# Talking-heads attention into a squared-ReLU feed-forward: three score blocks, eight gather tiles, and first loads in two batches

## The chip, the cores and the metric

The kernel runs on one core of one Trainium2 chip. The metric is device time in microseconds (us). A profiled execution also gives a trace; its span is the time from the first to the last instruction, a little less than the device time.

## The reference

There are 8 batches of 12 heads, 448 queries and keys, and a head dimension of 64. Attention mixes heads twice: the scores of the 12 heads are mixed by w_pre ahead of the softmax, and the softmax by w_post after it. A feed-forward layer with squared ReLU follows (768 to 2048 to 768).

```python
scores = scale * np.matmul(q, k.transpose(0, 1, 3, 2))
scores = np.einsum('bhij,hg->bgij', scores, w_pre)
attn = softmax(scores)                                  # over keys
attn = np.einsum('bhij,hg->bgij', attn, w_post)
x = np.matmul(attn, v).transpose(0, 2, 1, 3).reshape(B * S, H * D)
h = np.maximum(x @ w_in, 0.0)
out = h * h @ w_out
```

## The kernel before

**Data.** A score block holds 120 (the last of a batch: 88) queries of all 12 heads, queries on partitions. Mixing heads needs heads on partitions, so each tile of 10 queries is gathered: a DMA (gather, L344) copies 10 rows of 12 heads from the score block `S` to 120 partitions of a gather tile `G`. A batch has 45 such tiles in four blocks of 12, 12, 12 and 9.

**One iteration.** The main loop runs over `ds`, two tiles at a time, 180 times and two more. In this text, iteration n is the pass with ds = n. Tiles are numbered through all batches, so iteration n mixes tiles 2n and 2n + 1, and batch 1 starts with tile 45. An iteration issues, in this order:

- the loads due (POOL's DMA queue; `at_load(i, ...)` is due when i is 2 ds or 2 ds + 1)
- timed units, such as `av_unit` (attention times v: ot_ps, L195)
- `unmix` of two tiles (L385): w_post is applied with the softmax tile `d` as the weights; DVE copies the result to `at` (L390). It stands LAG = 2 iterations behind mix
- in three iterations per batch `turn_unit` (L178): q and k of a later batch are transposed on PE and copied by DVE and ACT (L182)
- `scores_for`: score pairs, two heads each. `score_pair` runs 4 matmuls (L324) and two copies into the block, one on ACT and one on DVE (L327)
- `mix` (L353): w_pre is applied to two gather tiles. ACT takes the exponential with its sum (L358), DVE the reciprocal (L360), POOL scales it into a `d` tile (L362)
- `gathers_for`: the gathers that are due
- `spin` in the first ten iterations: matmuls without use that keep PE busy
- `fill`: units of the feed-forward of an earlier batch, from a list `filler`: `ffn1_unit` (h_ps, L246; ACT or DVE takes the ReLU, POOL or DVE the square, L258) and `ffn2_unit` (o_ps, L279; DVE copies it, L286 or L291, and SP's queue stores it, L269 or L294). Their share per iteration is set by the code's weights and not by the lines that change.

The order on PE and POOL is that of the code, since the loop stands in a manual schedule. Each other engine also works in the order in which its instructions were issued. PSUM has eight banks, taken in turn by all units.

**What paces scores and gathers.** There are 32 blocks of 6 pairs. `needs(step)` says how many pairs must have been issued for a tile. `gathers_for(ds)` issues gathers up to tile 2 ds + AHEAD + 1, with AHEAD = 10, and stops at a tile whose block isn't complete. There are AHEAD + 2 = 12 gather tiles, used in turn. `scores_for` sets how many pairs are wanted from the block that the gathers are in, with cases of its own for the first twelve iterations and for the turn from batch 0 to batch 1 (`FIRST_TURN`), and issues one or two per iteration. Score blocks have two buffers (`bufs=2`). The third block of batch 0 is held in a third place, the tile that later takes the second half of the weights w_out (`shared_half`, w2_1), so the loads of that half stand after its gathers.

**Queues.** POOL issues all loads of q, k, v and weights; these are DMAs that also cast, on queue q0 of the profile. Gathers go on SP's queue (q1), in batch 0 every second one on ACT's (q10). SP also issues the stores. A DMA from SP or ACT waits, before it is issued, for the eighth DMA before it from those two, as these share eight semaphores; POOL's have eight of their own.

**Start.** q and k of batch 0 are loaded and turned, and six pairs are issued as the parts arrive. Then come the first gathers (tiles 0 to 9), six more pairs, a spin of 8 rounds (32 matmuls), and all loads marked -1: four parts of v (192 KB each) and eight of w_in (`w1`, 384 KB each).

Of the kernel before, what the change touches and what calls it, by code (L numbers as in the profile page):

```python
# [1 line left out]

# [6 lines left out]
BF16 = mybir.dt.bfloat16  # L9
# [14 lines left out]
NT = 45  # L24
# [6 lines left out]
TW = TQ + 2  # L31
PARTS = [[0, 16, 32, NT], [0, 15, 31, NT]]
LAG = 2
AHEAD = 10
OFF = 64 - H * (IQ // 2)
SCALE = 1.0 / 8.0
FIRST_TURN = (15, 16, 17)
# [6 lines left out]
def kernel(  # L44
# [76 lines left out]
    onesblk = consts.tile([P, 64], BF16, name="onesblk")  # L121
    nc.vector.memset(onesblk[:, :], 1.0)

    ND = 2 * LAG + 4
    DW = S + PR
    dts = [consts.tile([P, DW], BF16, name=f"d{x}") for x in range(ND)]
    for t in dts:
# [14 lines left out]
    half2 = FT // 2 * DMODEL  # L142
    w2 = {0: wts.tile([P, half2], BF16, name="w2_0")}

    def shared_half():
        return wts.tile([P, half2], BF16, name="w2_1", tag="w2_1", bufs=1)

    def w2_part(x):
        return w2[x][:, :].rearrange("p (c m) -> p c m", m=DMODEL)


    qTs, kTs, bvecs, xts, h2ts, ats = {}, {}, {}, {}, {}, {}

# [77 lines left out]

    def load_w2(x):
        n = DFF // 8
        c = x % 4 * 2
        if x == 4:
            w2[1] = shared_half()
        nc.gpsimd.dma_start(out=w2_part(x // 4)[:, c:c + 2, :],
                            in_=moe_w_out[n * x:n * x + n, :].rearrange("(c p) m -> p c m", p=P))

    def ffn1_unit(b, ft, half, c0=0, c1=S):  # L240
        if half == 0:
            h_open[0] = bank("h_ps")
        ps = h_open[0]
        n = c1 - c0
        for c2 in range(3 * half, 3 * half + 3):
            nc.tensor.matmul(ps[:, 0:n], lhsT=w1[ft // 4][:, c2, ft % 4 * 128:ft % 4 * 128 + 128],  # L246
                             rhs=xts[b][:, c2, c0:c1], start=(c2 == 0), stop=(c2 == NPAIR - 1))
        if half == 0:
            return
        if (b, ft) not in h2ts:  # L250
            h2ts[(b, ft)] = ffnp.tile([P, S], BF16, name="h2", tag="h2", bufs=FT + 1)
        hr = ffnp.tile([P, S], F32, name="hr", tag="hr", bufs=2)
        if n < S and ft % 2:
            nc.vector.tensor_scalar_max(out=hr[:, 0:n], in0=ps[:, 0:n], scalar1=0.0)
        else:
            nc.scalar.activation(out=hr[:, 0:n], in_=ps[:, 0:n], func=ACT.Relu)  # L256
        square = nc.vector if n < S and ft % 4 else nc.gpsimd
        square.tensor_tensor(out=h2ts[(b, ft)][:, c0:c1], in0=hr[:, 0:n], in1=hr[:, 0:n], op=ALU.mult)  # L258

    h_open, o_open, osbs = {}, {}, {}  # L260
# [11 lines left out]
    def ffn2_unit(b, mt, nt, part):  # L272
        if part == 0:
            o_open[(b, mt, nt)] = bank("o_ps")
        ps = o_open[(b, mt, nt)]
        for ft in range(4 * part, 4 * part + 4):
            for n2 in ((nt,) if mt < 3 else (0, 1)):
                dst = ps[:, 0:384] if mt < 3 else ps[64 * n2:64 * n2 + 64, 0:384]
                nc.tensor.matmul(dst, lhsT=h2ts[(b, ft)][:, mt * 128:mt * 128 + ROWS[mt]],  # L279
                                 rhs=w2_part(ft // 8)[:, ft % 8, n2 * 384:(n2 + 1) * 384], start=(ft == 0), stop=(ft == FT - 1))  # L280
        if part < 3:
            return
        if mt < 3:
            if nt == 0:
                osbs[b] = ffnp.tile([P, DMODEL], F32, name="osb", tag="osb", bufs=2)
            nc.vector.tensor_copy(out=osbs[b][:, 384 * nt:384 * nt + 384], in_=ps[:, 0:384])  # L286
            if nt == 1:
                store_rows(b, mt, osbs[b])
        else:
            osb = ffnp.tile([P, 384], F32, name="osb3", tag="osb3", bufs=1)  # L290
            nc.vector.tensor_copy(out=osb[:, :], in_=ps[:, 0:384])  # L291
            r, p = divmod(128 * mt, PR)
            for n2 in range(2):
                nc.sync.dma_start(out=out_rows[b, r, p:p + 64, n2 * 384:(n2 + 1) * 384],  # L294
                                  in_=osb[64 * n2:64 * n2 + 64, :])
# [15 lines left out]
    def score_pair(n):  # L311

        b, blk, p = n // (4 * NPAIR), n // NPAIR % 4, n % NPAIR
        if (b, blk) not in Sb:
            if (b, blk) == (0, 2):
                Sb[(b, blk)] = shared_half()[:, 0:H * S].rearrange("p (h s) -> p h s", s=S)
            else:
                Sb[(b, blk)] = work.tile([P, H, S], BF16, name="S", tag="S", bufs=2)
        pss = [bank("s_ps") for _ in range(2)]
        for hh in range(2):  # L320
            rs = slice(64 * hh, 64 * hh + 64)
# [14 lines left out]
    def gather(k):  # L336

        b, t = steps[k]
        blk, tl = divmod(t, TPB)
        n = min(IQ, S - IQ * t)  # L340
        x = BLK_OFF[blk] + IQ * tl
        g = gts[k % len(gts)]
        eng = nc.scalar if b == 0 and k % 2 else nc.sync
        eng.dma_start(out=g[OFF:OFF + H * n, :], in_=Sb[(b, blk)][x:x + n, :, :])  # L344
        Gs[k] = g

# [72 lines left out]
    with tc.manual_schedule(engines={PE, POOL}):  # L419
# [12 lines left out]
        for x in range(2):  # L432
            at_load(-1, load_w1, x)
        for x in range(4):
            at_load(-1, load_v, 0, x)
            at_load(44 + x, load_v, 1, x)
        for x in range(2, 8):
            at_load(-1, load_w1, x)
        for x in range(8):
            at_load(18 + 2 * x + (6 if x > 3 else 0), load_w2, x)  # L440
        for x in range(6):
            at_load(6 + 2 * x, load_qk, 1, x)
            at_load(46 + 2 * x, load_qk, 2, x)
        for b in range(1, B):
            if b + 2 < B:
                for x in range(6):
# [2 lines left out]
                for x in range(4):  # L449
                    at_load(NT * b + 34 + 2 * x, load_v, b + 1, x)  # L450
        nd = len(steps) // 2
        issued, gathered = [2 * NPAIR], [0]
        blocks = [(b, blk) for b in range(B) for blk in range(4)]
        starts = [NT * b + TPB * blk for b, blk in blocks] + [len(steps)]

        def scores_for(ds, most):
            tile = 2 * ds + AHEAD + 2
            blk = sum(tile >= x for x in starts) - 1
            if blk + 1 >= len(blocks):
                want = NPAIR * len(blocks)  # L460
            elif ds < 2 * NPAIR:
                want = 2 * NPAIR + 1 + ds
            elif blk in (3, 4):
                want = NPAIR * 4 + 2 * max(0, ds - FIRST_TURN[0])
            else:
                into, size = tile - starts[blk] - 2, starts[blk + 1] - starts[blk] - 2
                want = NPAIR * (blk + 1) + -(-NPAIR * into // size)
            want = min(want, issued[0] + most, NPAIR * min(blk + 2, len(blocks)))
            k = min(2 * ds + 8, len(steps) - 1)
            want = max(want, needs(steps[k]))  # L470
            while issued[0] < want and issued[0] % NPAIR < turned.get(issued[0] // (4 * NPAIR), 0):
                score_pair(issued[0])
                issued[0] += 1
# [6 lines left out]
                gathered[0] += 1  # L480

        gathers_for(-1)
        for n in range(NPAIR, 2 * NPAIR):
            score_pair(n)
        spin(8)
        for f in loads.get(-1, []):
            f()
        for ds in range(nd + LAG):
# [82 lines left out]
```

## Time and profile before

| What | Before |
|---|---|
| median of 4 runs | 610.61 us (609.32 to 612.82) |
| profiled execution: its time / its span | 608.88 / 607.1 us |
| busy PE / DVE / ACT / POOL | 554.4 / 426.0 / 412.2 / 396.9 us |
| mean granted PE clock | 0.979 |
| DMA | 74.99 MB, mean 124 GB/s |
| gathers G<-S | 105 KB each; SP takes 0.78 us to issue one, ACT 0.80 us |

PE is TensorE, DVE is VectorE, ACT ScalarE, POOL GpSimd and SP SyncE; PEld is PE's weight load. An engine's line is shown as "start, length, engine, line, operation, tile written <- tiles read, count [idle time before it <- what ended that]". An engine can be idle at no cost when it isn't the one that sets the end. A queue's share is the time that its packets took, as a share of the 16 DMA engines in the stretch; it can sum to over 1, as packets of several queues are under way at once. Granted clock is a share of full speed.

### The profile page before, as it was taken

How to read it: one execution, taken by the hardware profiler on the slowest of the kernel's cores; microseconds unless marked ns; L12 is line 12 of the kernel's file. 1: busy time of each engine (PE TensorE's matmuls, PEld its weight loads, DVE VectorE, ACT ScalarE, POOL GpSimd, SP SyncE). 2: the span in 40 equal slices, each digit the busy share in tenths (PEclk: the TensorE clock that was granted, in tenths of full speed). 3: DMA queues.
4: the chain of work that ended last, by engine and by line, in shares of the span. 5: the costliest groups of instructions: out<-in, count | busy, mean ns of one | idle time of the engine just before them, and what ended most of it. 6: DMA issues, size and time to landing. Idle time of an engine off the chain costs nothing.

```text
span 607.1 us, 28400 instructions
## 1 busy us (share of the span) xinstructions
PE 554.4 (91%) x11922; PEld 313.6 (52%) x11922; DVE 426.0 (70%) x1104; ACT 412.2 (68%) x1217; POOL 396.9 (65%) x587
## 2 busy tenths in 40 slices
PE   3698787789899999999999999999999999999997
PEld 1365555545455455545555455545555555555554
DVE  5488697988787777786787687777777777755101
ACT  3377575676689767886688667886688767962420
POOL 7278556557468954997469944996468845892440
PEclk9899797999899999999999999999999999999999
DMA  9999769669555786388546785388544665432103
GB/s 137 226 199 215 152 108 175 123 102 170 131 116 119 137 157 138 66 152 148 121 109 116 143 160 131 62 166 137 127 100 87 111 151 119 79 66 56 38 11 81
DMA packets 83364, 74.99 MB, mean 124 GB/s; under 512 B 6436, under 2 KB 80164, under 8 KB 83236
## 3 DMA queue, kind: packets, MB, share of 16 engines
q1 hardware_dynamic: 48982, 47.20, 33.0%
q0 software_dynamic: 31264, 23.60, 28.6%
q10 hardware_dynamic: 2990, 2.37, 1.2%
q8 instruction: 93, 1.52, 1.0%
q14 instruction: 35, 0.29, 0.1%
HBM read 47.20 MB, written 11.01 MB: 96 GB/s over the span
## 4 chain that ended last, share of the span: by engine, by line
PE 67%; POOL 9%; DVE 9%; DMA 5%; ACT 4%; issue 2%; ACTq 0%; DVEq 0%
PE o_ps L279 24%; PE h_ps L246 17%; PE at_ps L385 8%; PE ot_ps L195 7%; PE m_ps L353 5%; DVE at L390 5%; DMA G<-S 4%; POOL d L362 4%; POOL h L258 3%; PE s_ps L324 3%; PE tr_ps L178 2%; ACT e_sb L358 2%; ACT xt L206 1%; POOL qkst L71 1%; DVE S L327 1%
## 5 line engine op out<-in xcount | busy, mean ns | idle before, releaser
L362 POOL TENSOR_SCALAR d<-e_sb,rc 128x448 bf16<-128x448 f32 x360 | 228.1, 645 | 164.9 <-DVE rc L360 163.2
L390 DVE CAST at<-at_ps 128x480 bf16<-128x480 f32 x360 | 219.8, 650 | 58.9 <-PE at_ps L385 53.7
L358 ACT ACTIVATE e_sb<-m_ps 128x448 f32<-128x448 f32 x360 | 196.0, 559 | 13.9 <-PE m_ps L353 6.5
L246 PE MATMUL h_ps<-xt,w 128*128 128x448 bf16 (+2 forms) x960 | 164.6, 319 | 2.1 <-DVE at L390 0.7
L279 PE MATMUL o_ps<-w,h 128*128 128x384 bf16 (+1 forms) x1024 | 162.9, 329 | 0.9 <-ACT xt L206 0.5
L327 ACT CAST S<-s_ps 128x448 bf16<-128x448 f32 x186 | 96.4, 542 | 54.5 <-PE s_ps L324 33.0
L246 PEld LDWEIGHTS <-w 128*128 128x128 bf16 x960 | 80.7, 99 | 77.7 <-issue 27.8
L279 PEld LDWEIGHTS <-h 128*128 128x128 bf16 (+1 forms) x1024 | 83.0, 101 | 71.9 <-issue 26.9
L258 POOL TENSOR_TENSOR h<-hr 128x448 bf16<-128x448 f32 (+2 forms) x124 | 108.7, 884 | 17.1 <-ACT hr L256 17.1
L327 DVE CAST S<-s_ps 128x448 bf16<-128x448 f32 x186 | 110.8, 614 | 4.6 <-DMA G<-S 4.6
L353 PE MATMUL m_ps<-G,pre 64*64 64x448 bf16 x720 | 82.0, 360 | 13.5 <-DVE at L390 3.3
L385 PEld LDWEIGHTS <-d 60*64 60x64 bf16 x5760 | 64.6, 109 | 55.6 <-issue 31.4
L385 PE MATMUL at_ps<-post,d 60*64 60x60 bf16 x5760 | 85.5, 195 | 6.8 <-POOL d L362 3.2
L256 ACT ACTIVATE hr<-h_ps 128x448 f32<-128x448 f32 (+2 forms) x136 | 68.8, 514 | 23.5 <-PE h_ps L246 11.2
L360 DVE RECIPROCAL rc<-sm 128x1 f32<-128x1 f32 x360 | 52.3, 156 | 39.9 <-ACT e_sb L358 37.8
L324 PE MATMUL s_ps<-kT,qT 64*64 64x448 bf16 x768 | 70.7, 372 | 9.2 <-ACT S L327 7.8
L358 ACT ACTIVATION_READ_ACCUMULATOR e_sb<-m_ps 128x1 f32 x360 | 78.5, 218 | 0.0
L206 ACT ACTIVATE xt<-ot_ps,bvec 128x160 bf16<-128x160 f32 (+3 forms) x144 | 44.8, 385 | 48.9 <-PE ot_ps L195 39.5
L286 DVE COPY osb<-o_ps 128x384 f32<-128x384 f32 x48 | 26.0, 547 | 39.9 <-PE o_ps L279 39.5
L195 PE MATMUL ot_ps<-at,v 128*64 128x160 bf16 (+4 forms) x1152 | 47.2, 233 | 5.1 <-ACT S L327 2.6
L195 PEld LDWEIGHTS <-v 128*64 128x64 bf16 x1152 | 39.6, 112 | 18.3 <-issue 17.6
L353 PEld LDWEIGHTS <-pre 64*64 64x64 bf16 x720 | 29.0, 107 | 33.5 <-issue 28.2
(43 smaller groups left out, 227.9 us busy)
## 6 DMA issues: line engine op xcount, KB each, us to landing
G<-S SPq DMA_DIRECT2D x324, 105.0 KB
out_dram<-osb SPq DMA_DIRECT2D x48, 192.0 KB
v<-in_v_dram POOLq DMA_DIRECT2D x32, 192.0 KB, 5.4
qkst<-in_k_dram POOLq DMA_DIRECT2D x24, 224.0 KB, 6.0
qkst<-in_q_dram POOLq DMA_DIRECT2D x24, 224.0 KB, 5.4
w<-in_moe_w_in_dram POOLq DMA_DIRECT2D x8, 384.0 KB, 18.4
w<-in_moe_w_out_dram POOLq DMA_DIRECT2D x8, 384.0 KB, 14.4
G<-S ACTq DMA_DIRECT2D x16, 105.0 KB
```

Source lines behind the costliest of these rows:

```text
L195: nc.tensor.matmul(ps[64 * hh:64 * hh + 64, TW * y + c0:TW * y + 2 + n], lhsT=vs[b][:, g, r, :], rhs=at[:, r, g, c0:2 + n], start=(y == 0 ...
L246: nc.tensor.matmul(ps[:, 0:n], lhsT=w1[ft // 4][:, c2, ft % 4 * 128:ft % 4 * 128 + 128], rhs=xts[b][:, c2, c0:c1], start=(c2 == 0), stop=( ...
L256: nc.scalar.activation(out=hr[:, 0:n], in_=ps[:, 0:n], func=ACT.Relu)
L258: square.tensor_tensor(out=h2ts[(b, ft)][:, c0:c1], in0=hr[:, 0:n], in1=hr[:, 0:n], op=ALU.mult)
L279: nc.tensor.matmul(dst, lhsT=h2ts[(b, ft)][:, mt * 128:mt * 128 + ROWS[mt]], rhs=w2_part(ft // 8)[:, ft % 8, n2 * 384:(n2 + 1) * 384], sta ...
L324: nc.tensor.matmul(pss[hh][z:z + 64, 0:S], lhsT=qTs[b][rs, p, q0:q0 + 64], rhs=kTs[b][rs, p, :], start=True, stop=True)
L327: copy(out=Sb[(b, blk)][:, 2 * p + hh, :], in_=pss[hh][:, 0:S])
L353: nc.tensor.matmul(pss[y][64 * x:64 * x + 64, 0:S], lhsT=pre[rows, :], rhs=gs[x][rows, :], start=True, stop=True)
L358: nc.scalar.activation(out=e[:, :], in_=pss[y][:, 0:S], func=ACT.Exp, scale=SCALE, accum_out=sm[:, 0:1])
L362: nc.gpsimd.tensor_scalar(out=d[:, 0:S], in0=e[:, :], scalar1=rc[:, 0:1], scalar2=-1.0 / S, op0=ALU.mult, op1=ALU.add)
L385: nc.tensor.matmul(us[x][PR * z:PR * z + PR, c:c + HR], lhsT=d[rows, j:j + PR], rhs=post[rows, :], start=True, stop=True)
L390: nc.vector.tensor_copy(out=dst, in_=src)
```

## The change

It has these parts:

- `S` has three buffers. w_out lies in four tiles of its own, so no score block shares its place.
- AHEAD goes from 10 to 6, so there are 8 gather tiles. The number of `d` tiles goes from 8 to 6. The tile osb3 is gone; the last rows use the tile osb.
- Scores are paced by `place(tile)`, the pair count, with fractions, that belongs to a tile's place in its block, taken at tile 2 ds + AHEAD + LEAD (20 ahead). The special cases are gone. Two pairs are issued in an iteration when the issue is behind by more than 1.5 (2 where a timed unit stands), else one, and never more than three blocks from the one being gathered.
- Nine pairs are issued ahead of the loop where there were twelve, and six gathers where there were ten. The first spin has 4 rounds.
- ACT issues only gathers 1 and 3.
- Of the loads marked -1 only two parts of w1 and two of v remain. The others are due in iterations 1 to 4, those of q and k of batch 1 from iteration 4 (before: 3), and those of w_out one per iteration from 10 to 17 (before: 9 to 12 and 16 to 19).
- The squares of batch 0 go to DVE for ft % 2, where they went for ft % 4; so 8 of 16 and not 4 of 16 are POOL's in each part of the batch.

```diff
-AHEAD = 10
+AHEAD = 6
+LEAD = 14
...
-    ND = 2 * LAG + 4
+    ND = 2 * LAG + 2
...
-    w2 = {0: wts.tile([P, half2], BF16, name="w2_0")}
...
+    w2 = [wts.tile([P, FT // 4, DMODEL], BF16, name=f"w2_{x}") for x in range(4)]
...
-        square = nc.vector if n < S and ft % 4 else nc.gpsimd
+        square = nc.vector if n < S and ft % 2 else nc.gpsimd
...
-            osb = ffnp.tile([P, 384], F32, name="osb3", tag="osb3", bufs=1)
-            nc.vector.tensor_copy(out=osb[:, :], in_=ps[:, 0:384])
+            osb = ffnp.tile([P, DMODEL], F32, name="osb", tag="osb", bufs=2)
+            nc.vector.tensor_copy(out=osb[:, 0:384], in_=ps[:, 0:384])
...
-            if (b, blk) == (0, 2):
-                Sb[(b, blk)] = shared_half()[:, 0:H * S].rearrange("p (h s) -> p h s", s=S)
-            else:
-                Sb[(b, blk)] = work.tile([P, H, S], BF16, name="S", tag="S", bufs=2)
+            Sb[(b, blk)] = work.tile([P, H, S], BF16, name="S", tag="S", bufs=3)
...
-        eng = nc.scalar if b == 0 and k % 2 else nc.sync
+        eng = nc.scalar if k in (1, 3) else nc.sync
...
-            at_load(-1, load_v, 0, x)
+            at_load(-1 if x < 2 else 2, load_v, 0, x)
             at_load(44 + x, load_v, 1, x)
         for x in range(2, 8):
-            at_load(-1, load_w1, x)
+            at_load(1 + x, load_w1, x)
+        for x in range(6):
+            at_load(9 + 2 * x, load_qk, 1, x)
+            at_load(46 + 2 * x, load_qk, 2, x)
         for x in range(8):
-            at_load(18 + 2 * x + (6 if x > 3 else 0), load_w2, x)
-        for x in range(6):
-            at_load(6 + 2 * x, load_qk, 1, x)
-            at_load(46 + 2 * x, load_qk, 2, x)
+            at_load(20 + 2 * x, load_w2, x)
...
-        issued, gathered = [2 * NPAIR], [0]
+        issued, gathered = [NPAIR + 3], [0]
...
-        def scores_for(ds, most):
-            tile = 2 * ds + AHEAD + 2
+        def place(tile):
             blk = sum(tile >= x for x in starts) - 1
             if blk + 1 >= len(blocks):
-                want = NPAIR * len(blocks)
-            elif ds < 2 * NPAIR:
-                want = 2 * NPAIR + 1 + ds
-            elif blk in (3, 4):
-                want = NPAIR * 4 + 2 * max(0, ds - FIRST_TURN[0])
-            else:
-                into, size = tile - starts[blk] - 2, starts[blk + 1] - starts[blk] - 2
-                want = NPAIR * (blk + 1) + -(-NPAIR * into // size)
-            want = min(want, issued[0] + most, NPAIR * min(blk + 2, len(blocks)))
-            k = min(2 * ds + 8, len(steps) - 1)
-            want = max(want, needs(steps[k]))
+                return NPAIR * len(blocks)
+            return NPAIR * (blk + (tile - starts[blk]) / (starts[blk + 1] - starts[blk]))
+
+        def scores_for(ds, most):
+            want = math.ceil(place(2 * ds + AHEAD + LEAD))
+            full = sum(gathered[0] >= x for x in starts) - 1
+            want = min(want, issued[0] + most, NPAIR * min(full + 3, len(blocks)))
+            want = max(want, needs(steps[min(2 * ds + 4, len(steps) - 1)]))
...
-        for n in range(NPAIR, 2 * NPAIR):
+        for n in range(NPAIR, issued[0]):
             score_pair(n)
-        spin(8)
+        spin(4)
...
-                scores_for(ds, 2 if ds < NT // 2 or not now and ds % 3 == 0 else 1)
+                behind = place(2 * ds + AHEAD + LEAD) - issued[0]
+                scores_for(ds, 2 if behind > (2 if now else 1.5) else 1)
```

More of the change, by code (lines that the diff above doesn't have):

```diff
@@ L1 @@
+import math
 from contextlib import ExitStack
@@ L141 @@
     w1 = [wts.tile([P, NPAIR, DFF // 4], BF16, name=f"w1_{x}") for x in range(4)]
-    half2 = FT // 2 * DMODEL
-    w2 = {0: wts.tile([P, half2], BF16, name="w2_0")}
[L145 to L149, printed above, removed]
+    w2 = [wts.tile([P, FT // 4, DMODEL], BF16, name=f"w2_{x}") for x in range(4)]
     qTs, kTs, bvecs, xts, h2ts, ats = {}, {}, {}, {}, {}, {}
@@ L233, in load_w2 @@
         n = DFF // 8
[L234 to L237, printed above, removed]
+        c = x % 2 * 2
+        nc.gpsimd.dma_start(out=w2[x // 2][:, c:c + 2, :],
                             in_=moe_w_out[n * x:n * x + n, :].rearrange("(c p) m -> p c m", p=P))
@@ L279, in ffn2_unit @@
                 nc.tensor.matmul(dst, lhsT=h2ts[(b, ft)][:, mt * 128:mt * 128 + ROWS[mt]],
-                                 rhs=w2_part(ft // 8)[:, ft % 8, n2 * 384:(n2 + 1) * 384], start=(ft == 0), stop=(ft == FT - 1))
+                                 rhs=w2[ft // 4][:, ft % 4, n2 * 384:(n2 + 1) * 384], start=(ft == 0), stop=(ft == FT - 1))
         if part < 3:
@@ L294, in ffn2_unit @@
                 nc.sync.dma_start(out=out_rows[b, r, p:p + 64, n2 * 384:(n2 + 1) * 384],
-                                  in_=osb[64 * n2:64 * n2 + 64, :])
+                                  in_=osb[64 * n2:64 * n2 + 64, 0:384])
     def ffn1_units(b, c0=0, c1=S):
```

## The prediction

> **What bounds the kernel now.** I read the busy time by stretches first, then the waits of TensorE (PE), the chain of waits and the queues. Columns of the stretches: stretch, its length, then busy us (instructions) of PE, weight loads, DVE, ACT, POOL, then granted clock, DMA share, GB/s.
>
> ```profile
> 0.00:20.00 20.00, 9.38 (x242) 5.36 (x246) 13.27 (x49) 7.49 (x12) 13.45 (x25) 1.00 1.06 152
> 20.00:40.00 20.00, 13.62 (x326) 8.87 (x318) 9.43 (x27) 11.41 (x34) 8.66 (x15) 0.83 1.06 216
> 40.00:60.00 20.00, 16.53 (x490) 11.36 (x485) 17.60 (x52) 15.62 (x51) 16.42 (x26) 1.00 1.10 216
> ...
> 80.00:100.00 20.00, 15.14 (x318) 10.53 (x319) 17.27 (x48) 11.96 (x39) 12.33 (x20) 0.93 0.86 143
> ...
> 300.00:400.00 100.00, 97.75 (x2202) 52.68 (x2190) 75.56 (x188) 79.44 (x233) 72.94 (x106) 1.00 0.62 122
> ```
>
> From about 160 us to 550 us PE is 97 to 99% busy at full clock. What is left to win lies ahead of that: PE idles some 30 us before 160 us, part of it at a lower clock, while the DMA engines are full for the first 60 us. A delay removed there moves the end by the same amount, since PE then works through a fixed list. The longest pieces of the chain (start, length, what) show where the idle time is:
>
> ```profile
> 16.82 8.20 DMA G<-S
> ...
> 56.01 7.41 DMA G<-S
> ...
> 92.43 5.46 DMA G<-S
> ...
> 147.77 5.06 DMA G<-S
> ```
>
> All are gathers, but of two kinds. The first is mixing waiting for its first tiles. The last two are score copies that wait until a score block is free, as the waits there show:
>
> ```profile
> 98.21 0.53 ACT L327 CAST S<-s_ps 128x448 bf16<-128x448 f32 x1 [4.86 <-DMA G<-S]
> 98.79 2.50 PE L195 MATMUL ot_ps<-at,v 128*64 128x128 bf16 x43 [2.63 <-ACT S L327]
> ```
>
> ACT works in order: its score copy waits 4.86 us for a gather of the old block, and everything behind it, then PE, waits too. The same occurs at 152.93 (2.29 us on ACT, 1.99 us on PE).
>
> The queues, first from 24 to 36 us, then from 92 to 98 us (packets, MB, share of 16 engines):
>
> ```profile
> q0 software_dynamic: 1339, 1.32, 65.2%
> q1 hardware_dynamic: 764, 0.63, 20.3%
> q10 hardware_dynamic: 759, 0.63, 15.6%
> ```
> ```profile
> q0 software_dynamic: 1326, 0.70, 93.6%
> q1 hardware_dynamic: 486, 0.40, 23.7%
> ```
>
> q0 carries POOL's loads, q1 the gathers of SP, q10 those of ACT. With both q1 and q10, 12.7 gathers of 120 packets pass in 12 us: 0.95 us each. With SP alone beside loads, 4.05 pass in 6 us: 1.5 us each.
>
> **What the Trainium skill says.** "DMA: Bandwidth & Descriptors", Queues, rings and completion order: each DMA engine takes its rows in turn, packet by packet. The trace fits. A packet takes 65.2% x 192 / 1339 = 93 ns on q0, 51 on q1, 40 on q10. By the same page (Why a DMA increments its semaphore by 16) a gather from 10 score rows runs on 10 engines, so 12 packets on each: an estimate of 12 x (93 + 51 + 40) = 2.2 us for a pair of gathers; the trace has 1.9. For q1 alone, 92 to 98 us: 12 x (68 + 47) = 1.4 us per gather; the trace has 1.5. The section Issuing engines are not separate DMA queues says a second issuer saves issue time only; under load the two windows speak against that, as two rows get two turns. "TensorE: Matmul & The Clock Gate", What's actually happening: an idle PE falls to half clock. The trace has 12 h_ps matmuls (128x128) in 1.48 us after the wait at 98.8 us; before, 12 of 128x160 took 1.00.
>
> **The change part by part.** "Iteration" is one pass of the ds loop (two tiles). I count the mixes in the timeline: mix 0 starts at 26.46 us, 9 at 45.99, 10 at 49.63, 14 at 58.05, 15 at 63.55, 17 at 70.45, 22 at 87.76, 24 at 93.80, 25 at 102.30, 34 at 129.63, 43 at 154.05. Which pair and gather falls in which iteration follows from the arithmetic of scores_for and gathers_for.
>
> (a) First loads and ACT's queue. Before, ACT issues its fourth gather and is then held until 25.83 (ACTq 17.70, 8.13 us x4) as a DMA waits for an earlier one. Its next score copy starts at 25.87, mix 0 at 26.46. After, ACT issues two gathers, only six are started at once, and 6 w1 parts and 2 v parts are left for later. q0 then has 6 qk, 2 w1 and 2 v parts: 6 x 0.23 + 2 x 0.39 + 2 x 0.2 = 2.56 MB; the stretches moved 102 GB/s in the first 10 us and 201 in the next 10, so they end near 18 us. Gathers start at 16.82 as before and land in about 4.5 us (estimate; the chain's 5.06 and 5.46 had loads beside them): mix 0 at 21.3. Gain 5.2. Bounds 2 (only the ACT hold goes) and 6.
>
> (b) The same loads later, past POOL's queue and beside gathers. Iterations 1 to 4 issue v, v, w1 / w1, w1 / w1, w1 / w1, qk on POOL ahead of that iteration's two d (0.63 us each, L362). A load costs POOL 0.65 to 0.77 us. So POOL needs 2.1 + 1.3, 1.5 + 1.3, 1.5 + 1.3, 1.4 + 1.3 = 11.7 us for four iterations that took 2.0 each: by POOL alone, d of iteration 9 starts some 3.9 us earlier than now, 1.3 less than 5.2. Then the gathers: all but two go on q1 alone. While q0 has work, one takes 12 x (93 + 51) = 1.73 us, a pair 3.5, against iterations of 2.0. Eight tiles land before that starts, at about 24 us; tile 19 then lands at 24 + 12 x 1.73 = 45 and mix 9 starts near 46: all of (a) lost. In iterations 10 to 17 one w2 part is issued in each, where before four were in iterations 9 to 12. With w2 packets (76.8% x 208 / 1408 = 113 ns) a gather takes 1.97 us, and 16 of them 31.5: mix 17 at 77.5, 7 later than now. That is the far end (-12); the near end is -1.3. q0 is not always full (68.6% of the engines from 36 to 48 us, where qk parts came one by one), so I take -3.5.
>
> (c) Squares of batch 0: ft % 2 in place of ft % 4 moves 4 of 16 squares per part, 12 in all, from DVE (0.42 us) to POOL (0.45): 5 us off DVE, 9 to 10 of 10 us busy from 80 to 120 us; POOL has room there (5 to 7). A fifth of it on the path: +1 (0 to 2).
>
> (d) First gathers of batch 1. Before, tile 45 is gathered in iteration 19 (82.25 us), after it in iteration 20, as pairs come two at a time: pairs 28, 29 copied by about 85, landing 4.5 later at 89.5, mix 22 due at 87.76. DVE has fewer copies just before, so I take -1.3 (0 to -2.3).
>
> (e) Third score block. No pair now waits for its buffer: the first pair of a block comes five or more iterations after the last gather from the buffer it takes (before: one to three). The wait of 2.63 + 0.67 us before 98.8 goes and with it the slow clock, some 0.7: +4. Next due is the unmix of that iteration, whose d are ready. Likewise at 153.5: 1.99 and 2.61 for 1.41 us on 8 o_ps matmuls: +3. Both 0 at worst.
>
> (f) Third block of batch 1 (tiles 69 on). With pairs paced a block later, three turns (iterations 29 to 31) without any pair, and at most two per iteration, its last pair is issued in iteration 33, its gathers after that, and mix 34 needs tile 69: one iteration of lead. The pair's copies end near 128.4 (copies in iteration 33 run from 127.34 to 128.45), plus 4.5 is 133, due 129.63: -3.3, and 0.5 of clock: -3.8 (-2 to -5). SP's queue behind it holds gathers 70 to 73; mix 35 needs 71 a little later than it lands.
>
> (g) Gather tiles 12 to 8, LEAD, d tiles 8 to 6. A gather now has 4 mixes (11.6 us at 2.9 per iteration) from the free slot to its use; its 0.8 us issue twice, stores of 2 us ahead of it on SP and 5.5 us of landing make 9. Cost 0 by that cover; without it 0.5 us in each loaded iteration. d tiles: the sixth is freed by the unmix two iterations on: 0. osb3 joins osb: its buffer was stored eight o_ps units earlier: 0. Spin of 4 instead of 8: hidden in the wait for mix 0. w2 in four tiles: 0, used only from iteration 31.
>
> Sum: 5.2 - 3.5 + 1 - 1.3 + 4 + 3 - 3.8 = 4.6 with each part alone. Parts overlap (PE cannot be early and wait on DVE too), so I take 4.1. The profiled execution took 608.88 (span 607.1 and 1.8 around it): 604.8. The median of the runs is 610.61, 1.7 above it: **606.5**.
>
> **Rivals.**
> - More is kept (A): gathers keep pace in spite of one queue, as eight tiles lead and q0 is not full: (b) is -1.3, (f) -2. 4.1 + 2.2 + 1.8 = 8.1: 602.5. For it: q0 left room from 36 to 48 us. Against: DMA at 1.06 to 1.10 until 60 us.
> - Given back (B): (b) -7.5: 610.5. The waits only change place, from blocks to landings.
> - Slower (C): gathers starve on the one hardware queue from 24 to 75 us. (b) is -12: 4.1 - 8.5 = -4.4: 615. It decides from where a pair of gathers needs over 2.6 us through iterations 1 to 17. For it: 1.5 us per gather at 92 to 98 us. Against: qk parts come singly. If leads of three iterations also fail beside v and qk loads later (g), up to 620.
> - That the third block isn't what held the copies: then (e) is 0 and the result lies near B.
>
> **How the numbers follow.** Forecast 0.40 (604 to 609), A 0.22, B 0.14, C 0.24. A difference under 0.5% (3 us) can hardly be told from none. Faster: A and about two thirds of the forecast, 0.48; same: the rest of it and B, 0.28; slower: C, 0.24. The range 600 to 617 leaves out a tenth at each end.
>
> **What would show it.** (a) mix 0 near 21 us and no hold on ACT. (b) Mix 9 between 42 and 46, mix 17 between 66 and 78; PE waiting for gathers there means B or C. (e) No score copy waiting for a gather. (f) A wait of 3 us for a gather ahead of mix 34. (g) After 160 us PE 97% busy as before; waits for gathers there would make the forecast wrong, and so would a start not earlier than 24 us.

## The result, and the profile after

The changed kernel takes 614.07 us (median of 37 runs, 610.69 to 617.16), the kernel before 610.51 (median of 56 runs, 607.24 to 614.57). The ratio is 1.0057, with a 95% interval from 1.0045 to 1.007: slower by 3.6 us, where 606.5 was forecast. The profiled execution took 615.68 us (span 613.9), so it lies 1.6 us above the median, and that of before 1.6 below its own; the two traces differ by 6.8 us in span, the medians by 3.6.

The page of the changed kernel: its span and the row of the mix (busy us, mean ns, then idle time before it and the largest releaser).

```profile
span 613.9 us, 28388 instructions
...
L342 PE MATMUL m_ps<-G,pre 64*64 64x448 bf16 x720 | 85.2, 357 | 28.2 <-DMA G<-S 18.9
```

The same row of the kernel before:

```profile
L353 PE MATMUL m_ps<-G,pre 64*64 64x448 bf16 x720 | 82.0, 360 | 13.5 <-DVE at L390 3.3
```

PE is as busy as before in sum (554.1 and 554.4 us), and the line numbers have moved (mix L342, unmix L374, score copies L316). The mix now waits 18.9 us for gathers; before, its largest releaser was DVE, with 3.3. By stretches, with the columns of the prediction:

```profile
0.00:20.00 20.00, 8.63 (x224) 5.02 (x224) 11.24 (x41) 8.46 (x14) 7.89 (x17) 1.00 0.94 137
20.00:40.00 20.00, 13.41 (x310) 7.20 (x314) 10.04 (x28) 9.50 (x30) 15.12 (x23) 0.83 0.91 161
40.00:60.00 20.00, 14.80 (x421) 10.26 (x420) 14.56 (x41) 13.93 (x44) 11.98 (x20) 1.00 1.11 206
60.00:80.00 20.00, 13.67 (x398) 9.88 (x394) 13.16 (x36) 10.03 (x29) 13.66 (x23) 0.85 1.03 194
80.00:100.00 20.00, 16.77 (x401) 11.42 (x399) 17.29 (x42) 14.95 (x47) 11.95 (x22) 0.98 0.47 93
300.00:400.00 100.00, 96.72 (x2143) 53.05 (x2143) 73.92 (x185) 76.20 (x222) 67.74 (x98) 1.00 0.62 119
```

The kernel before from 60 to 80 us, beside the fourth line:

```profile
60.00:80.00 20.00, 15.12 (x450) 10.84 (x451) 14.28 (x40) 12.39 (x36) 10.72 (x18) 0.83 0.73 140
```

Look at the last two columns. In the first 40 us fewer bytes move than before (137 and 161 GB/s against 152 and 216), and between 60 and 80 us the DMA engines are full (share 1.03, before 0.73): work has been put off from the first stretches to the fourth. PE pays between 40 and 80 us, 28.5 us busy, where before had 16.53 there in the first half and 15.12 in the second (31.7). The last row shows a second loss that is small in each iteration but lasts long: PE is 96.7% busy where it was 97.8%.

The longest pieces of the chain of waits (start, length, what):

```profile
16.94 5.66 DMA G<-S
...
38.23 11.16 DMA G<-S
...
62.38 14.23 DMA G<-S
...
133.28 6.45 DMA G<-S
...
147.65 7.16 DMA G<-S
```

The gathers at 92 and 147 us that held score copies before are gone. In their place gathers hold the chain almost without a break from 27 to 77 us, and again at 133 and 147 us. There it is the mix that waits, and the score copies don't:

```profile
102.61 1.53 PE L189 MATMUL ot_ps<-at,v 128*64 128x128 bf16 x48
...
135.11 0.38 PE L342 MATMUL m_ps<-G,pre 64*64 64x448 bf16 x3 [0.82 <-DMA G<-S]
...
139.77 0.38 PE L342 MATMUL m_ps<-G,pre 64*64 64x448 bf16 x3 [1.39 <-DMA G<-S]
...
154.85 0.38 PE L342 MATMUL m_ps<-G,pre 64*64 64x448 bf16 x3 [1.59 <-DMA G<-S]
```

The attention units (L189) that stood behind a score copy at 98.79 us now start without a wait. The other three lines show a mix whose first tile is there and whose second isn't.

Mix starts in the two traces show where time is won and lost (us; after minus before):

| Mix | Before | After | Difference | What lies in between |
|---|---|---|---|---|
| 0 | 26.46 | 22.65 | -3.8 | first loads, ACT's queue |
| 2 | 32.14 | 26.92 | -5.2 | |
| 9 | 45.99 | 48.01 | +2.0 | loads moved into iterations 1 to 4; one queue |
| 14 | 58.05 | 62.78 | +4.7 | loads of q, k, w2 |
| 18 | 75.35 | 82.31 | +7.0 | loads of w2 |
| 24 | 93.80 | 100.56 | +6.8 | first gathers of batch 1 |
| 25 | 102.30 | 104.54 | +2.2 | the wait for a score block that is gone |
| 31 | 120.81 | 123.24 | +2.4 | |
| 36 | 135.14 | 142.08 | +6.9 | tiles 69 and on |
| 41 | 146.91 | 152.91 | +6.0 | |
| 44 | 158.22 | 162.31 | +4.1 | the second such wait |
| 47 | 165.24 | 168.75 | +3.5 | |
| 179 | 550.95 | 557.75 | +6.8 | the steady part |

So the start is earlier by 5.2 us, 12.2 us are lost by mix 18, 4.5 come back at mix 25, 4.5 are lost by mix 36, 1.9 come back by mix 44, and 3.3 go in the steady part. One trace of a kernel is not its median: a version that differs only in the squares (c3 below), with the same median to 0.3 us, lost 9.8 us between mix 2 and mix 18, and a3 9.2. The loss there is 9 to 12 us.

Where the 12.2 us come from is seen in the stretches 16:20, 20:25 and 25:30 us. First before, then after:

```profile
16.00:20.00 4.00, 3.90 (x50) 2.03 (x46) 3.91 (x8) 1.46 (x4) 1.93 (x3) 1.00 1.43 198
20.00:25.00 5.00, 0.61 (x16) 0.25 (x5) 0.00 (x0) 0.00 (x0) 0.35 (x1) 1.00 1.21 235
25.00:30.00 5.00, 3.54 (x33) 1.76 (x36) 1.08 (x4) 3.43 (x9) 0.63 (x2) 0.53 1.19 244
```
```profile
16.00:20.00 4.00, 3.27 (x32) 1.71 (x27) 3.06 (x6) 2.54 (x6) 0.00 (x0) 1.00 0.81 116
20.00:25.00 5.00, 2.35 (x28) 1.24 (x32) 0.40 (x3) 1.28 (x5) 0.97 (x2) 0.79 0.48 105
25.00:30.00 5.00, 4.70 (x132) 2.71 (x124) 3.80 (x10) 3.85 (x12) 4.96 (x8) 0.86 0.89 142
```

Before, every compute engine nearly stands still from 20 to 25 us, but 235 GB/s move. After, the engines work and the DMA engines are half empty, as POOL issues no load until it has scaled the first `d` tiles at 24.03 us. Over these 14 us the bytes that didn't move are (198 - 116) x 4 + (235 - 105) x 5 + (244 - 142) x 5 = 1,488 KB, or 1.49 MB. At the 206 GB/s of 40 to 60 us they would take 7.2 us when they come later, beside gathers; this is an estimate.

### The profile page after: what moved, and what is told of

It reads as the page before. It is cut to its first block, busy times and chain, and to the rows that moved or that the text cites. A ratio compares the mean times of both kernels' runs of the same rounds, so it can differ in the third digit from the quotient of the medians.

```text
span 613.9 us, 28388 instructions
## 1 busy us (share of the span) xinstructions
PE 554.1 (90%) x11906; PEld 313.1 (51%) x11906; DVE 423.9 (69%) x1086; ACT 413.3 (67%) x1217; POOL 401.5 (65%) x599
## 3 DMA queue, kind: packets, MB, share of 16 engines
q0 software_dynamic: 31264, 23.60, 28.5%
## 4 chain that ended last, share of the span: by engine, by line
PE 62%; DMA 11%; POOL 10%; DVE 8%; ACT 4%; issue 3%; ACTq 0%; DVEq 0%; SPq 0%
PE o_ps L271 21%; PE h_ps L238 17%; DMA G<-S 11%; PE at_ps L374 7%; PE ot_ps L189 6%; PE m_ps L342 5%; POOL d L351 4%; DVE at L379 4%; POOL h L250 4%; PE s_ps L313 2%; ACT e_sb L347 2%; POOL qkst L73 2%; PE tr_ps L172 2%; ACT xt L200 1%; DVE S L316 1%
## 5 line engine op out<-in xcount | busy, mean ns | idle before, releaser
L316 ACT CAST S<-s_ps 128x448 bf16<-128x448 f32 x192 | 99.3, 542 | 39.1 <-PE s_ps L313 35.6
L250 POOL TENSOR_TENSOR h<-hr 128x448 bf16<-128x448 f32 (+2 forms) x136 | 114.1, 847 | 17.1 <-ACT hr L248 17.1
L316 DVE CAST S<-s_ps 128x448 bf16<-128x448 f32 x192 | 114.3, 613 | 1.3 <-PE s_ps L313 1.3
L342 PE MATMUL m_ps<-G,pre 64*64 64x448 bf16 x720 | 85.2, 357 | 28.2 <-DMA G<-S 18.9
L374 PEld LDWEIGHTS <-d 60*64 60x64 bf16 x5760 | 63.6, 109 | 57.9 <-issue 29.9
L374 PE MATMUL at_ps<-post,d 60*64 60x60 bf16 x5760 | 84.9, 194 | 8.6 <-POOL d L351 5.0
L248 ACT ACTIVATE hr<-h_ps 128x448 f32<-128x448 f32 (+2 forms) x136 | 68.6, 513 | 25.4 <-PE h_ps L238 11.8
L313 PE MATMUL s_ps<-kT,qT 64*64 64x448 bf16 x768 | 68.5, 367 | 1.9 <-issue 1.0
L342 PEld LDWEIGHTS <-pre 64*64 64x64 bf16 x720 | 30.7, 106 | 52.6 <-issue 43.2
L189 PE MATMUL ot_ps<-at,v 128*64 128x160 bf16 (+4 forms) x1152 | 46.8, 232 | 1.4 <-DVE at L379 1.4
L189 PEld LDWEIGHTS <-v 128*64 128x64 bf16 x1152 | 39.4, 111 | 14.6 <-issue 14.0
## 6 DMA issues: line engine op xcount, KB each, us to landing
w<-in_moe_w_in_dram POOLq DMA_DIRECT2D x8, 384.0 KB, 10.4
w<-in_moe_w_out_dram POOLq DMA_DIRECT2D x8, 384.0 KB, 11.0
```

Source lines behind the costliest of these rows:

```text
L189: nc.tensor.matmul(ps[64 * hh:64 * hh + 64, TW * y + c0:TW * y + 2 + n], lhsT=vs[b][:, g, r, :], rhs=at[:, r, g, c0:2 + n], start=(y == 0 ...
L313: nc.tensor.matmul(pss[hh][z:z + 64, 0:S], lhsT=qTs[b][rs, p, q0:q0 + 64], rhs=kTs[b][rs, p, :], start=True, stop=True)
L316: copy(out=Sb[(b, blk)][:, 2 * p + hh, :], in_=pss[hh][:, 0:S])
L342: nc.tensor.matmul(pss[y][64 * x:64 * x + 64, 0:S], lhsT=pre[rows, :], rhs=gs[x][rows, :], start=True, stop=True)
L374: nc.tensor.matmul(us[x][PR * z:PR * z + PR, c:c + HR], lhsT=d[rows, j:j + PR], rhs=post[rows, :], start=True, stop=True)
```

## Experiments

At the start there were four theories. Q: the gathers of batch 0 starve since all but two go on one hardware queue beside POOL's loads. L: the loads' bytes, moved to stand beside the gathers, cost the time, whatever the queues. T: eight gather tiles in place of twelve leave too little lead. F: the pairs, which are paced anew and of which none is issued in a turn, come late. Each kernel below is the changed kernel with the edit shown, except for b1 and d3, which start from the kernel before. Ratios are to the kernel before; differences in us are between medians where no trace is named.

**a1, two queues for the gathers of batch 0.**

```diff
-        eng = nc.scalar if k in (1, 3) else nc.sync
+        eng = nc.scalar if b == 0 and k % 2 else nc.sync
```

> The changed kernel, with every second gather of batch 0 issued by ACT again; nothing else. Theory Q (one hardware queue gets one turn per load packet): two queues get two turns, a pair of gathers takes about 2.1 us beside loads and not 3.2; mix 9 starts near 43 us (48.0 in the changed kernel), mix 17 near 69 to 71 (75.6), and the time falls by 4 to 6 us. Rival L (the loads put later and close together fill the DMA engines, whatever the queue): mix 17 stays within 1.5 us and the time within 2. Rival T (8 gather tiles in place of 12 are the cause): no change either.

Measured: 608.74 us, 0.9982 (0.9964 to 1.0), which is 5.3 below the changed kernel. Mix 9 starts at 43.45, mix 17 at 72.03, mix 18 at 78.31. The queues from 36 to 48 us (packets, MB, share of 16 engines), in the changed kernel and then in a1:

```profile
q0 software_dynamic: 1943, 1.86, 93.4%
q1 hardware_dynamic: 989, 0.82, 26.2%
```
```profile
q0 software_dynamic: 1759, 1.66, 84.8%
q1 hardware_dynamic: 652, 0.54, 18.9%
q10 hardware_dynamic: 621, 0.51, 15.5%
```

A gather is 130 packets, 120 of 896 bytes and 10 of 4 bytes (its 105 KB are 0.1075 MB). So 989 packets are 7.6 gathers, 1.58 us each; 652 + 621 are 9.8 gathers, 1.23 us each, with nearly the same loads beside them (1.86 and 1.66 MB). It repeats: with one queue a2, a3, c2 and c3 also pass 7.6 in these 12 us (c4, whose score copies wait, 6.9), and c1, with two, 10.0. So a second queue takes a larger share for the gathers, as Q says; T alone, with no change, is not what came. But it isn't all: from mix 2 to mix 9 a1 loses 3.4 us where the changed kernel loses 7.2; from mix 9 to mix 18 it loses 5.5 where the changed kernel loses 4.9.

In the trace the wait has mostly moved: from mix 2 to mix 18 PE waits for no gather in a1, but POOL waits 6.3 us for earlier loads of its own before it can issue the next, and PE waits 4.4 us for POOL's `d`. This stretch takes 52.1 us in a1, and 53.0 in c3, where PE waits 10.5 us for gathers. Where the 5.3 us of the medians lie this trace can't show: its run took 612.36 us, 3.6 over a1's median, and it is no faster than c3's trace at mix 47 (165.54 and 164.90) or at mix 179 (554.42 and 553.95).

**a2, w_out's loads after mix 18.**

```diff
-            at_load(20 + 2 * x, load_w2, x)
+            at_load(36 + 2 * x, load_w2, x)
```

> The changed kernel, with the eight parts of w_out due in iterations 18 to 25 and not 10 to 17; their first use is in iteration 31. Theory Q: with POOL's queue empty of them a gather takes about 1 us in iterations 10 to 17, so mix 17 starts near 70 (75.6), of which one or two us come back later as the same loads then stand beside gathers; net 2 to 4 us faster. Rival L: the same loads cost the same later, net within 1 us. Rival T: no change.

Measured: 614.87 us, 1.0108 (1.0074 to 1.0142): no gain. The queues from 60 to 72 us, in the changed kernel and then in a2:

```profile
q0 software_dynamic: 1195, 1.68, 85.2%
q1 hardware_dynamic: 787, 0.65, 21.2%
```
```profile
q1 hardware_dynamic: 1655, 1.37, 48.7%
q0 software_dynamic: 41, 0.03, 1.6%
```

Without loads 12.7 gathers pass on the same single queue, 0.94 us each, against 6.1, 1.98 us each. Mix 18 starts 8.8 us sooner, and by mix 30 (119.50 us, 0.6 later than in the changed kernel) all of it is given back, beside other loads. The rate is what Q says, and the outcome what L says: the bytes have to pass somewhere in the first 120 us. T, which expected no change, fits the outcome too.

**a3, a pair in the iterations with a turn.**

```diff
             if ds in turns:
...
-                scores_for(ds, 0)
+                scores_for(ds, 1)
```

> The changed kernel, with one score pair allowed in an iteration that turns q and k, where there was none. The third block of batch 1 is then complete in iteration 31 and not 33. Theory F (its gathers come one iteration ahead of their use): the waits for gathers between mix 31 and mix 36 go, mix 36 starts 2 to 4 us earlier relative to mix 31, and the time falls by 2 to 4 us. Rival: the gathers there are late for another reason (loads of batch 3 beside them); within 1 us.

Measured: 602.54 us, 0.9894 (0.9871 to 0.9917), 11.5 below the changed kernel, and the largest gain of any single edit: far more than expected. Against the trace of the changed kernel it is 4.7 us ahead at mix 24, 8.4 at mix 36 and 12.8 at the end. Of the 4.7, 3.3 are there at mix 18, as c3's trace has 2.9 there with only the squares changed, so these can't be put down to the edit. What can: from mix 19 to mix 22 a3 takes 8.3 us where the changed kernel takes 9.4, and from mix 31 to mix 36 14.8 where it takes 18.8. These are gathers of batch 1 that come sooner, as F says. The last part lies in the steady part, which no theory had named: from mix 47 to 179 the changed kernel takes 389.0 us, a3 384.0. These lengths repeat from trace to trace: 388.6 to 389.4 in the changed kernel, a1, a2, c2, c3 and c5, 383.8 to 384.3 in a3, c1, d1 and d2, which have this edit. In 15 of the 132 iterations the changed kernel issues two pairs where a3 issues one; these are longer by 7.3 us in all, 0.2 to 0.9 each. The others are shorter by 2.4 in all. One of the fifteen in the changed kernel, on PE:

```profile
245.57 0.55 PE L313 MATMUL s_ps<-kT,qT 64*64 64x448 bf16 x8
245.95 0.35 PE L342 MATMUL m_ps<-G,pre 64*64 64x448 bf16 x2
246.56 0.38 PE L342 MATMUL m_ps<-G,pre 60*64 60x448 bf16 x2 [0.26 <-DVE osb L283]
247.13 1.29 PE L238 MATMUL h_ps<-xt,w 128*128 128x448 bf16 x6 [0.19 <-DVE at L379]
```

Eight score matmuls stand in a row, and the mix behind them waits for DVE: each unit takes the next PSUM bank, and DVE, with two pairs to copy, hasn't emptied it. That wait over 165 to 545 us, in the changed kernel and then in a3 (us, times, longest):

```profile
PE m_ps L342 <- DVE at L379: 3.1, 12, 0.4
```
```profile
PE m_ps L342 <- DVE at L379: 1.1, 5, 0.3
```

It accounts for 2 of the 5 us; for the other 3 no single wait is shown. No mix waits for a gather in this stretch in either.

**b1, the kernel before with one queue.**

```diff
-        eng = nc.scalar if b == 0 and k % 2 else nc.sync
+        eng = nc.scalar if k in (1, 3) else nc.sync
```

> The kernel before, with ACT issuing only gathers 1 and 3 and SP the rest; nothing else. Theory Q: mix 0 a little earlier as ACT is not held, then 1.6 us per gather beside loads: mix 14 near 64 to 68 us (58.0), and the time 4 to 8 us over the kernel before. Rival L: within 2 us. Rival T: with 12 gather tiles the gathers keep ahead of the mixes, so within 2 us too.

Measured: 611.73 us, 1.0029 (1.0011 to 1.0046): 1.2 us slower, where Q expected 4 to 8; L and T, which said within 2 us, fit. Mix 14 is 3.7 us later than before, but mix 18 is on time (75.37 and 75.35): the kernel before has slack between these, since SP then waits for the pairs of batch 1 (from 68.4 to 82.25 us) and gathers that are behind catch up. One queue alone is thus not the cause; it costs where there is no slack behind it.

**c1, a1 and a3 together.** Both edits.

> The changed kernel with both earlier edits: every second gather of batch 0 on ACT, and one score pair allowed in a turning iteration. If the two losses are separate (gathers beside loads up to iteration 17, late blocks of batch 1 and later), the gains add: 614.1 less 5.3 less 11.5 is 597 to 598. If both cure the same lateness, it stays near the better of the two, 601 to 603.

Measured: 601.82 us, 0.9865 (0.9825 to 0.9904). That is 0.7 below a3, where a1 alone gained 5.3: the gains overlap.

**c2, w_out's loads in two groups, as before.**

```diff
-            at_load(20 + 2 * x, load_w2, x)
+            at_load(18 + 2 * x + (6 if x > 3 else 0), load_w2, x)
```

> The changed kernel with the parts of w_out due as in the kernel before: four in iterations 9 to 12, four in 16 to 19, not one per iteration from 10 to 17. Theory Q: the bytes are the same and SP has no pause in its gathers here in which they could pass, so mix 18 stays within 2 us of 82.3 and the time within 2 us. Rival P (their place in time is what costs): mix 18 starts 3 to 5 us earlier and the time falls by as much.

Measured: 611.92 us, 1.0027 (1.0008 to 1.0046), 2.2 below the changed kernel. Mix 18 starts at 79.55, within 0.1 us of c3's, which doesn't touch these loads; so the trace can't place the 2.2 us.

**c3, the squares as before.**

```diff
-        square = nc.vector if n < S and ft % 2 else nc.gpsimd
+        square = nc.vector if n < S and ft % 4 else nc.gpsimd
```

> The changed kernel with the squares of batch 0 as before (4 of 16 on POOL, not 8). By the prediction's step (c) 1 us slower (0 to 2). Rival: DVE is not what ends iterations 11 to 30 while gathers lag; within 1 us.

Measured: 613.74 us, 1.0057 (1.0041 to 1.0073), within 0.4 us of the changed kernel. DVE's 5 us of squares cost nothing that can be told.

**c4, two score blocks.**

```diff
-            Sb[(b, blk)] = work.tile([P, H, S], BF16, name="S", tag="S", bufs=3)
+            Sb[(b, blk)] = work.tile([P, H, S], BF16, name="S", tag="S", bufs=2)
...
-            want = min(want, issued[0] + most, NPAIR * min(full + 3, len(blocks)))
+            want = min(want, issued[0] + most, NPAIR * min(full + 2, len(blocks)))
```

> The changed kernel with two score buffers, and pairs allowed two blocks ahead, not three; the order of pairs moves by two iterations at most. Theory E (the third buffer is what ended the waits of score copies): copies wait for gathers again near iterations 26, 38 and 44, and the time rises by 4 to 8 us. Rival: the new pace alone keeps pairs off a block that is still gathered; within 1.5 us.

Measured: 626.13 us, 1.0264 (1.0228 to 1.03), 12 above the changed kernel and more than expected. The waits of score copies for gathers are back, such as this on ACT:

```profile
114.30 0.53 ACT L316 CAST S<-s_ps 128x448 bf16<-128x448 f32 x1 [3.77 <-DMA G<-S]
```

The three-block kernels have none of these waits. But the 12 us are not what the third block wins over the kernel before: the longest wait in c4 (5.57 us on ACT, at 34.11 us) is for the third block of batch 0, which had a place of its own before, and c4 passes from mix 24 to mix 25 in 3.98 us, as the changed kernel does. So the new pacing needs the third block; the wait at mix 25 went with either number of blocks.

**c5, no pause in the first loads.**

```diff
-            at_load(-1 if x < 2 else 2, load_v, 0, x)
+            at_load(-1, load_v, 0, x)
...
-            at_load(1 + x, load_w1, x)
+            at_load(-1, load_w1, x)
```

> The changed kernel with all parts of v and w_in issued at the start again, as in the kernel before. Theory Q: mix 0 starts later, near 25 us (22.7), since gathers stand behind them from the first, but POOL's queue runs empty by 34 us, gathers then take 1 us, and mix 9 starts near 44 to 46 (48.0): 1 to 4 us faster in all. Rival A (the pause is a gain that is kept): mix 9 after 49 and 2 to 4 us slower.

Measured: 610.64 us, 1.0003 (0.9977 to 1.003), 3.4 below the changed kernel. The stretches 20:25 and 25:30 us:

```profile
20.00:25.00 5.00, 1.75 (x20) 1.62 (x24) 0.16 (x1) 1.00 (x4) 0.07 (x1) 0.78 1.20 239
25.00:30.00 5.00, 4.22 (x123) 3.18 (x115) 2.93 (x8) 3.39 (x12) 2.62 (x5) 0.88 1.20 226
```

The DMA engines are full again (239 and 226 GB/s against 105 and 142), and mix 0 starts at 23.25, 0.6 later than in the changed kernel's trace. That trace is a late one, though: the other seven with the pause start mix 0 at 20.62 to 22.70, and d1 and d2, without it, at 24.81 and 23.65. So the pause gives about 2 us of the earlier start, and the end of ACT's hold the 2.4 that b1 has with two gathers on ACT and nothing else (mix 0 at 24.05). Mix 18 starts at 76.04, 6.3 earlier than in the changed kernel's trace and 3.4 earlier than in c3's, with gathers still on one queue and w_out's loads still in one row.

**d1, a3 and c5 together.** Both edits.

> The changed kernel with a pair allowed in turning iterations and with all parts of v and w_in at the start (no pause). If the two losses are separate: 614.1 less 11.5 less 3.4 is 599. If pairs in turns had already taken back what late gathers cost: 601 to 603.

Measured: 601.35 us, 0.9853 (0.9816 to 0.989), 1.2 below a3: overlap again, and the two intervals overlap too, so the 1.2 can't be told from none. Mix 2 starts at 28.91 us, 2.4 later than in a3's trace, and mix 18 at 79.36, 0.4 later: by mix 18 the pause has cost nothing here.

**d2, a1, a3, c2 and c5 together.** All four edits.

> The changed kernel with pairs in turns, no pause, every second gather of batch 0 on ACT, and w_out in two groups. Theory Q: the gathers of batch 0 no longer lag, mix 18 starts near 74 to 76 us; 596 to 600, the fastest. Rival: with no pause ACT is held again and the rest overlaps; 601 to 604.

Measured: 598.69 us, 0.9809 (0.9777 to 0.9841): 15.4 below the changed kernel and 11.8 below the kernel before, the fastest of all. Its stretches 20:40 and 60:80 us:

```profile
20.00:40.00 20.00, 14.72 (x363) 10.96 (x364) 10.98 (x33) 11.85 (x37) 9.63 (x16) 0.83 1.06 212
...
60.00:80.00 20.00, 16.13 (x437) 11.62 (x434) 14.33 (x36) 13.58 (x40) 11.02 (x19) 0.83 0.75 146
```

212 GB/s early, as before, and a share of 0.75 late. Mix 18 starts at 75.32, as before (75.35), with mix 2 3.4 us ahead; so even here the head start is gone by mix 18, but nothing beyond it. The 11 us over the kernel before all come later: 6.4 by mix 25, 9.1 by mix 47.

**d3, the kernel before with a pair in the iterations with a turn.** The edit of a3.

> The kernel before with one pair allowed in turning iterations. Theory F and its steady part (two pairs in one iteration delay the copies by some 0.4 us each): before has its doubled pairs too, after 160 us it gains 1 to 2 us; but the waits for a free score block come earlier by as much as pairs do, so in all between 3 us faster and 2 slower. Rival (turns were the whole loss of the changed kernel, and only of it): within 1 us.

Measured: 609.69 us, 0.9986 (0.9969 to 1.0002): no difference that can be told. From mix 47 to 179 its trace takes 384.8 us, where before and b1 take 385.7 and 385.5. So the rule for turns, which is old, costs some 0.9 us there under the old pacing, against 5 under the new.

## Why the prediction was wrong

What came about is the rival that was called slower (C, 615), with step (g) lost on top.

**(a) First loads and ACT's queue: right.** Predicted +5.2 with mix 0 at 21.3; measured 3.8 at mix 0 (22.65) and 5.2 at mix 2. The eight traces with these first loads have mix 0 between 20.62 and 22.70. Both reasons hold: the hold on ACT is gone (2.4 us by b1), and the shorter first loads give about 2 us more (c5, d1 and d2 against the eight).

**(b) The same loads later: the step that failed.** The term was -3.5, with -12 as the far end; it measured -12.2 in the trace, -9.8 in c3's. The mechanism was named, gathers beside loads; the size was wrong. The far end was worked out with q0 always full, and then taken down to -3.5 for the gaps that q0 had had from 36 to 48 us (68.6%). But in the kernel before those gaps were there because most of w1 and all of v had passed by 32 us (q0's share is 79.3% from 24 to 32 us, 36.9% from 32 to 36). The change moves just these loads behind that point, and q0 is at 93.4% from 36 to 48 us. Counting bytes from mix 2 to mix 18 shows what the stage had to do:

| Kernel | Mix 2 | Mix 18 | us between | MB between | GB/s | PE waits for gathers, us |
|---|---|---|---|---|---|---|
| before | 32.14 | 75.35 | 43.2 | 8.20 | 190 | 2.6 |
| b1, before with one queue | 28.87 | 75.37 | 46.5 | 8.70 | 187 | 6.0 |
| d2, all four | 28.70 | 75.32 | 46.6 | 8.87 | 190 | 1.4 |
| c5, no pause | 27.32 | 76.04 | 48.7 | 9.51 | 195 | 3.4 |
| d1, no pause, pairs in turns | 28.91 | 79.36 | 50.5 | 9.67 | 192 | 4.5 |
| a1, two queues | 26.19 | 78.31 | 52.1 | 10.57 | 203 | 0 |
| a3, pairs in turns | 26.56 | 78.97 | 52.4 | 10.37 | 198 | 7.3 |
| c3, squares | 26.43 | 79.45 | 53.0 | 10.49 | 198 | 10.5 |
| after | 26.92 | 82.31 | 55.4 | 10.81 | 195 | 11.6 |
| a2, late w2 | 26.11 | 73.49 | 47.4 | 8.05 | 170 | 6.8 |

With w_out's loads in place all of these, and c1, c2, c4 and d3 too, pass 187 to 203 GB/s at a DMA share of 0.94 to 1.09, so the time goes mainly with the bytes. a2 takes 2.8 MB out of this stage, and mix 18 starts 8.8 us sooner. The changed kernel reaches mix 2 5.2 us sooner, but with 3.50 MB behind it where the kernel before has 5.89. So 2.6 MB more stand between mix 2 and mix 18, and at 195 GB/s these take 13.4 us (an estimate; 12.2 measured). b1 and d2, which start mix 2 3.3 and 3.4 us sooner, lose just that by mix 18. All this is read from one trace of each kernel.

Rival C came near (615), but its reason, one hardware queue, is only a part: in the traces with two queues the waits for gathers go, and yet the stretch is only 0.5 to 3.3 us shorter (a1 against c3 and the changed kernel, c1 against a3). So it may be partly luck that packet turns on one queue gave the right far end.

The single queue decides how the engines are shared meanwhile: 1.58 us a gather, 1.23 with two. The section Queues, rings and completion order of "DMA: Bandwidth & Descriptors", in the Trainium skill, says that a DMA engine goes round the rows that have work; a1's two rows in place of one agree with it. In the medians two queues are worth 5.3 us, no pause 3.4, w_out's loads in two groups 2.2, and with a3 in place the first two only 0.7 and 1.2; these overlap and can't be summed. How the 12.2 us divide among them isn't settled: without the pause mix 18 is 3.4 to 6.3 us earlier in c5, and not earlier at all in d1. Nor is it settled what holds both the kernel before and d2 at 75.3 us, since their DMA share is only 0.73 and 0.75 from 60 to 80 us and PE hardly waits for gathers. T is not the cause where loads and queues stand as before, as d2 has eight gather tiles too and waits only 1.4 us; the changed kernel with twelve was not run.

Two sums of this step are off, without much effect. A gather has 130 packets, not 120, so the two windows have 11.7 and 3.7 gathers, 1.02 and 1.6 us each. And 11.7 us of POOL in place of 8.0 are 3.7 lost, not the 1.3 of the near end, unless POOL makes up the rest later, which the prediction doesn't show.

**(c) Squares:** predicted +1 (0 to 2). c3 is 0.3 us faster than the changed kernel, where 1 slower was expected; the intervals of the two can't tell this from none.

**(d) First gathers of batch 1:** predicted -1.3. The difference goes from +5.4 at mix 19 (84.90 against 79.49) to +6.6 at mix 22: -1.2. Right; the traces with pairs in turns take 8.0 to 8.3 us here, like the kernel before (8.3), the others with the new pacing 9.1 to 9.4.

**(e) Third score block:** predicted +4 and +3. The first is right: 4.5 at mix 25. Of the second, 3.9 came back between mix 42 and mix 44, but 2.0 had been lost just ahead, at mix 41 to 42, where the line at 154.85 us shows a mix waiting for its tile: 1.9 net from mix 41. The waits of score copies for gathers are gone, but the third block isn't shown to be the reason at mix 25: c4, with two blocks, has the same 3.98 us there under the new pacing, and waits at other places (mixes 3, 26 and 38). (For the clock, both groups of 12 matmuls that the prediction timed are 128x160: 1.48 us after the wait, 1.00 before it.)

**(f) Third block of batch 1:** predicted -3.8 with a wait of 3 us ahead of mix 34. Measured -4.5 from mix 31 to 36, with waits of 0.82 and 1.39 us at mixes 34 and 35 and the rest around them. a3, which issues pairs in the turns, takes 4.1 of it away, and c1, d1 and d2 do the same (14.8 to 15.5 us from mix 31 to 36, against 18.8). Right in size and cause; but the wait is spread over mixes 34 to 36, where one of 3 us ahead of mix 34 was forecast.

**(g) Gather tiles, LEAD, `d` tiles: predicted 0, measured -3.3.** This is a second step that failed. I costed only the buffers, and these do cost nothing: no mix waits for a gather from 165 to 545 us. What I missed is in the same edit: the rule that says when two pairs are issued. After a turn without pairs it makes them up two at a time, in iterations that then lack DVE's time and PSUM banks. a3 turns the 3.3 lost into 1.7 gained against before (384.0, before 385.7). Why the kernel before, with the same turns, suffers so little (d3) isn't shown. It issues two pairs about as often in this part (in 21 iterations up to mix 165, the changed kernel in 22), but never in an iteration with a timed unit; that rule wasn't tried by itself.

The sum by measured steps: +5.2 - 12.2 + 0 - 1.2 + 4.5 + 1.9 - 4.5 - 3.3 = -9.6, and the places between them in the table, which gave +2.8, make the -6.8 of the traces. With (b) at -3.5 and (g) at 0 the change would have gained, as forecast.

## What to carry to other kernels

Where the DMA share is near 1, count the bytes that a stage has to have by its end and what a change moves ahead of it: compute that starts sooner with fewer bytes behind it is a loan, and it is paid back at the loaded rate. A buffer that ends a wait is worth as much as the next resource in line allows, so look at the arrival of data behind it. When work is taken out of some iterations, look at the rule that makes it up: two units in one iteration can cost more than one in each, even with PE 97% busy and no data late.

## What was not expected of the hardware

Two hardware queues carry more gathers beside loads than one. Under "DMA: Bandwidth & Descriptors", Issuing engines are not separate DMA queues, the Trainium skill says that more issuers save issue time only; here 9.8 gathers against 7.6 pass in 12 us (a1) beside 1.66 and 1.86 MB of loads, and the measurement decides. Issue time was not what was saved, as 7.6 issues of 0.78 us fill 5.9 of the 12 us. A gather of 105 KB takes at most 0.94 us on one queue alone, 1.58 beside loads of w1 and q, k, and 1.98 beside those of w_out, so the same list of gathers can take twice the time without any change to itself.
